# Windowed attention with a linear bias, then a gated layer, on one core: keys in blocks of 32 and four heads to a tile of scores

## The chip, the cores and the metric

The kernel runs on 1 core of one Trainium2 chip. The metric is the device time of the whole program in microseconds (us); lower is better. The engines are TensorE (PE in the profile; PEld is its weight loads), VectorE (DVE), ScalarE (ACT), GpSimd (POOL) and SyncE (SP, which here issues most of the DMAs).

## What is computed

Inputs are q, k and v of shape 4 x 8 x 768 x 64 (batch, heads, sequence, head width), two matrices `moe_w_in` (512 x 1024) and `moe_w_out` (1024 x 512) and a gain `moe_g_ln` of 1024. With `n_global` = 8 and `n_local` = 96:

```
scores = q k^T / 8 - slope(head) * distance        # slope(h) = 2^-(h+1)
keep   = (key < 8) or (0 <= query - key < 96)      # everything else is masked
a      = softmax(scores);   x = a v                # per head, then x as 3072 tokens x 512
h      = x @ w_in;          solu = h * softmax(h)
y      = layernorm(solu) * g_ln;   out = y @ w_out # 3072 x 512, float32
```

A query thus sees at most 96 neighbours and 8 global keys, so that only a band of the 768 x 768 scores has to be computed.

## The kernel before

The program is written out engine by engine. Every piece of work is a *step* (`step(...)`, with its engine, dependencies and buffers); tables of numbers (`ORDER`, `SLOTS`, `ENGS`, `WARM`) give the order in which the steps are issued, the buffer that each takes, the engine where there is a choice, and some matmuls on a constant tile that only keep PE busy at the start. Within one engine, and in SP's queue of DMAs, everything runs in that order.

For each of the 4 batches:

- **Loads.** k and q of a pair of heads come in on SP (`load_heads`, or `load_rows` in runs of 256 bytes), are cast to 16 bits on POOL, DVE or ACT, turned on PE (`turn_k`, `turn_q`, L785: 6 matmuls against the identity) and evacuated on DVE or ACT into `kT`, `qT`. The pairs in `DMAT` (all four of batch 3) are turned by a DMA instead (L829). v comes in on SP (`load_v`) and is cast.
- **Scores.** Keys are cut into blocks of `BLK` = 64. A block's keys are met by `WIN` = 160 queries (64 + 96). A step `scores` takes one pair of heads and 6 blocks: 64 keys of one head on PSUM partitions 0 to 63 and of the other head on 64 to 127, even blocks in one bank, odd blocks in the next (`par`). TensorE is split into four tiles of 64 x 64 (L941). A batch has 8 such steps, 960 columns each for blocks 0 to 5 and 896 for blocks 6 to 11. In batch 0 the bias is added by matmuls with `identb` and `bw` (L927); in batches 1 to 3 (`FACT`) it is multiplied in afterwards by a table `fb` (L959, DVE or POOL). `exp` (L949, ACT) reads both banks at once and writes `eb`.
- **Units.** The 768 queries are cut into two units of 384. For each: scores of the global keys (`gscores`, `gexp` into `eg`), sums over the keys (`sums`, L1027 and L1037: 128 x 32 tiles, one band of 32 partitions for each pair), their logarithm (`ln`, ACT, 384 columns), a split into a high and a low part (`l16`, DVE, L1051), spread over the partitions (`spread`, L1073) and `rexp` (L1085, ACT), which gives the reciprocal.
- **Products with v.** For each duo of pairs (4 heads), `av1` and `av2` (L1121, 64 x 64 tiles) go into one `big` (two PSUM banks). In `av1` two of the tiles take the even blocks and two the odd ones, in `av2` the other way round; a small DVE copy, `tick` (L1129), stands between them. Then `xT` (L1141, DVE) multiplies by the reciprocal into `xT`.
- **The layer.** For each tile of 128 tokens (24 of them): `gemm1` (L1174, 8 matmuls of 512 columns), `ef` (L1180, ACT), `u` (L1183, DVE), squares (L1190 or L1194), a turn of `uu` either on PE (`turn_u`, L1209, evacuated by DVE or ACT) or, for the tiles in `TURNED`, by a DMA (L1199), then `gemm2` (L1266), a scaling (L1276 or L1279) and the store.

PSUM has 8 banks: `acc` is cut into 4 `big` of two banks, which are also used singly as `one`.

Of the kernel before, what the change touches and what calls it, by code (L numbers as in the profile page):

```python
# [18 lines left out]
P = 128  # L19
BLK = 64  # L20
WIN = 160
# [5 lines left out]
TURNED = set(range(5, 22))  # L27
HALVED = {23}
WORDS = {}
DMAT = {(3, p, n) for p in range(4) for n in "kq"}  # L30
# [32 lines left out]
"""  # L63
SLOTS = """
# [10 lines left out]
"""  # L75
ENGS = """
# [5 lines left out]
"""  # L82
WARM = """
20:2:13 32:2:5 45:2:2 54:2:1 82:0:3 100:0:1 110:6:1 139:5:1 171:4:2
# [58 lines left out]
def kernel(  # L143
# [25 lines left out]
    UW = 384  # L169
    RUN = S // P  # L170
    MG = NG + NL
    assert S == 768 and BLK + NL <= WIN and D == 64 and H * NG == 64
# [22 lines left out]
    bw = sb.tile([P, NPR, 3, WIN], FP16, name="bw")  # L195
# [5 lines left out]
    onesg = sb.tile([P, 2, NPR, 32], FP16, name="onesg")  # L201
# [12 lines left out]
    vgz = sb.tile([P, B, H, D], FP16, name="vgz")  # L214
    vt32 = sb.tile([P, B * NPR, D], FP32, name="vt32")
# [12 lines left out]
    v32 = many(3, [P, NBK, D], FP32, "v32_")  # L228
    v16 = many(2, [P, NBK, NPR, D], FP16, "v16_")
# [3 lines left out]
    eg = many(2, [P, UW // 2], FP16, "eg")  # L233
# [27 lines left out]
    def band(p):  # L261

        j = 2 * (p % 2) + p // 2
        return slice(32 * j, 32 * j + 32)

    HW = UW // 2

    def gband(r, p):

        o = 64 * r + 32 * (p // 2)  # L270
        return slice(o, o + 32)
# [13 lines left out]
    sl = sb.tile([P, NPR], FP32, name="sl")  # L285
    sf = sb.tile([P, NPR, 2], FP32, name="sf")
    dm = sb.tile([P, WIN], FP32, name="dm")
    fb = sb.tile([P, NPR, 2, GC], FP16, name="fb")
# [11 lines left out]
    def constants_iota():  # L300
        for hf in HALVES:
            nc.gpsimd.iota(ti[hf], pattern=[[1, WIN]], base=0,
                           channel_multiplier=-1)
            nc.gpsimd.iota(ri[hf, 0:1], pattern=[[0, 1]], base=0, channel_multiplier=1)
        nc.gpsimd.iota(tgm, pattern=[[1, MG]], base=0, channel_multiplier=0)
        nc.gpsimd.iota(ri[:, 1 : 1 + H], pattern=[[NG, H]], base=0, channel_multiplier=0)

    def constants_slopes():
        for p in range(NPR):
            for h, hf in enumerate(HALVES):  # L310
                nc.vector.memset(sl[hf, p : p + 1], -slopes[2 * p + h] / inv_sqrt_d / BSC)

    def constants_factor_slopes():
        for h, hf in enumerate(HALVES):
            for par in range(2):
                for p in range(NPR):
                    nc.gpsimd.memset(sf[hf, p, par : par + 1], -slopes[2 * p + (h ^ par)])

    def constants_factor():
        for p in range(NPR):  # L320
# [37 lines left out]
    def constants_rows():  # L358
        nc.vector.tensor_tensor(out=pick, in0=pick8[:, 0:H], in1=pick8[:, H : 2 * H], op=ALU.add)
        nc.vector.tensor_reduce(out=par4, in_=pick8.rearrange("r (x q l) -> r q x l", q=4, l=2),  # L360
                                axis=AX.XY, op=ALU.add)
        nc.vector.tensor_reduce(out=mlo, in_=pick8.rearrange("r (b l) -> r l b", l=2)[:, 1:2],
                                axis=AX.X, op=ALU.add)
        nc.vector.tensor_scalar(out=sgn, in0=mlo, scalar1=0.25, scalar2=-0.125,
                                op0=ALU.mult, op1=ALU.add)
# [14 lines left out]
    def constants_slr():  # L380
        for h in range(H):
            nc.gpsimd.memset(slr[:, h : h + 1], -slopes[h] * NL)
# [948 lines left out]
```

## Time and profile before

| | |
|---|---|
| time, median of 3 runs | 158.34 us (156.9 to 160.86) |
| the profiled execution | 158.12 us |
| its span, from first to last instruction | 156.5 us |
| busy PE / DVE / ACT / POOL | 144.1 / 119.9 / 123.8 / 51.9 us |
| matmuls | 1974 |
| granted TensorE clock | 1.0 throughout |

Busy time is the share in which at least one instruction of the engine is under way. Matmuls are pipelined and overlap, so a busy PE isn't a PE at its peak. In rows of groups, `x` is the count, then come the busy time in us and the mean duration of one in ns. The chain is the work that ended last, followed back step by step. The span is 1.62 us shorter than the time of the same execution.

### The profile page before, as it was taken

To read this page: it belongs to the slowest core of one execution; us is meant where nothing else is said; L and a number is where in the kernel's file an instruction comes from. 1 tells how busy PE (TensorE), PEld (TensorE's weight loads), DVE (VectorE), ACT (ScalarE), POOL (GpSimd) and SP (SyncE) were. 2 spreads that over 40 slices of the span, in tenths; PEclk is the share of its full clock that TensorE was granted. 3 is DMA by queue.
4 is the path that set the end of the run, shared out by engine and by line. 5 is a ranking of instruction groups with operands and counts; after the bars stand their busy time and mean duration, and the time that the engine had idled before them with its cause. 6 is when DMAs were issued, how large, how long until landed. Compare 5 with 4: busy or idle time off the path is not lost.

```text
span 156.5 us, 4929 instructions
## 1 busy us (share of the span) xinstructions
PE 144.1 (92%) x1974; PEld 76.3 (49%) x1974; DVE 119.9 (77%) x249; ACT 123.8 (79%) x214; POOL 51.9 (33%) x120
## 2 busy tenths in 40 slices
PE   6998986997898999999998999999989799999991
PEld 2455553456454546556544456454444454445460
DVE  6966553799879998889999997499777462788840
ACT  3389986999996999758996998989999546589712
POOL 7705714189438521734960000448301000000000
PEclk9999999999999999999999999999999999999999
DMA  4997899999969999999999899999999983054684
GB/s 157 335 351 178 288 311 397 366 272 329 266 161 264 213 202 294 204 275 201 219 239 176 182 237 216 164 263 135 215 225 290 211 316 133 4 113 89 188 315 168
DMA packets 74317, 35.83 MB, mean 229 GB/s; under 512 B 63344, under 2 KB 69816, under 8 KB 74296
## 3 DMA queue, kind: packets, MB, share of 16 engines
q1 hardware_dynamic: 73576, 34.36, 92.8%
q10 hardware_dynamic: 720, 1.18, 2.0%
q8 instruction: 15, 0.25, 0.6%
q14 instruction: 6, 0.05, 0.1%
HBM read 23.15 MB, written 6.29 MB: 188 GB/s over the span
## 4 chain that ended last, share of the span: by engine, by line
PE 34%; DMA 21%; DVE 16%; SPq 13%; ACT 7%; issue 4%; POOL 3%; DVEq 0%; ACTq 0%; POOLq 0%
PE acc L1266 11%; PE acc L1174 10%; SPq L537 5%; DVE uu L1183 5%; DMA x<-in_k_dram 4%; DVE eb L959 4%; DMA x<-in_q_dram 4%; DMA kT<-x 4%; DMA vgn<-vgn 4%; PE acc L1121 4%; DMA out_dram<-w_out 3%; DVE sqv L1194 3%; SPq L523 3%; SPq L1199 3%; PE acc L785 2%
## 5 line engine op out<-in xcount | busy, mean ns | idle before, releaser
L1174 PE MATMUL acc<-w_in_sb,xT 128*128 128x512 f16 x192 | 44.0, 380 | 1.3 <-POOL w_in_sb L279 1.3
L1266 PE MATMUL acc<-gw_out_sb,late 128*128 128x512 f16 (+1 forms) x200 | 44.7, 371 | 0.0
L1183 DVE SCALAR_TENSOR_TENSOR uu<-ef,acc 128x1024 f16<-128x1024 f16 x24 | 29.1, 1216 | 6.3 <-ACT ef L1180 4.5
L949 ACT ACTIVATE eb<-acc 128x960 f16<-128x960 f32 (+1 forms) x32 | 29.3, 944 | 1.3 <-PE acc L941 1.1
L1180 ACT ACTIVATE ef<-acc 128x1024 f16<-128x1024 f32 x24 | 24.6, 1025 | 6.9 <-PE acc L1174 6.1
L1174 PEld LDWEIGHTS <-xT 128*128 128x128 f16 x192 | 17.8, 98 | 21.5 <-DVE g L625 1.2
L1266 PEld LDWEIGHTS <-late 128*128 128x128 f16 x200 | 18.4, 98 | 20.1 <-issue 0.6
L279 POOL CAST x<-x 128x768 f16<-128x768 f32 x19 | 17.0, 898 | 30.0 <-DMA qT<-x 17.0
L1141 DVE TENSOR_TENSOR xT<-acc,rr 128x768 f16<-128x768 f32 x16 | 15.1, 954 | 5.9 <-ACT rr L1085 4.5
L1276 ACT ACTIVATE w_out<-acc,rstd 128x512 f32<-128x512 f32 (+1 forms) x19 | 12.7, 678 | 7.5 <-PE acc L1266 4.3
L1190 ACT ACTIVATE sqa<-uu 128x1024 f16<-128x1024 f16 x14 | 14.8, 1058 | 1.8 <-DVE uu L1183 1.7
L959 DVE TENSOR_TENSOR eb<-eb,fb 128x960 f16<-128x960 f16 (+1 forms) x21 | 14.8, 735 | 0.0
L1085 ACT ACTIVATE rr<-acc 128x768 f32<-128x768 f32 x16 | 12.2, 805 | 2.9 <-PE acc L1073 2.8
L785 PE MATMUL acc<-ident,x 128*128 128x128 f16 x144 | 11.3, 220 | 2.1 <-POOL x L279 1.1
L1194 DVE SCALAR_TENSOR_TENSOR sqv<-uu 128x1024 f16<-128x1024 f16 x10 | 12.6, 1265 | 0.1
L1121 PE MATMUL acc<-eb,v 64*64 64x160 f16 (+2 forms) x448 | 12.5, 217 | 0.0
L1292 PE MATMUL acc<-busy 128*128 128x512 f16 x29 | 10.3, 485 | 1.5 <-DVE busy L598 1.5
L785 PEld LDWEIGHTS <-x 128*128 128x128 f16 x144 | 8.6, 98 | 5.6 <-POOL x L279 1.5
L1121 PEld LDWEIGHTS <-v 64*64 64x64 f16 x448 | 10.2, 107 | 2.2 <-issue 1.7
L941 PE MATMUL acc<-qT,kT 64*64 64x160 f16 (+2 forms) x384 | 10.8, 227 | 0.3 <-ACT qT L275 0.3
L279 POOL CAST v<-v 128x704 f16<-128x704 f32 (+3 forms) x13 | 6.9, 555 | 11.9 <-DMA v<-in_v_dram 11.9
L1121 PE MATMUL acc<-eg,vgz 64*64 64x192 f16 x128 | 9.2, 257 | 0.0
(113 smaller groups left out, 189.1 us busy)
## 6 DMA issues: line engine op xcount, KB each, us to landing
x<-in_k_dram SPq DMA_DIRECT2D x16, 384.0 KB, 5.8
x<-in_q_dram SPq DMA_DIRECT2D x16, 384.0 KB, 4.8
out_dram<-w_out SPq DMA_DIRECT2D x19, 256.0 KB, 2.9
v<-in_v_dram SPq DMA_DIRECT2D x12, 192.0 KB, 5.3
late<-in_moe_w_in_dram SPq DMA_DIRECT2D x4, 512.0 KB, 4.5
w_out<-in_moe_w_out_dram SPq DMA_DIRECT2D x4, 512.0 KB
v<-in_v_dram SPq DMA_DIRECT2D x12, 160.0 KB, 3.4
v<-in_v_dram SPq DMA_DIRECT2D x12, 96.0 KB, 6.9
```

The lines of the kernel that those rows point to most:

```text
L279: nc.gpsimd.tensor_copy(out=out, in_=in_)
L785: nc.tensor.transpose(out=pt[:, ts(j, P)], in_=a[:, j], identity=ident)
L949: ex["fn"] = (lambda ex=ex, qk=qk, gw=gw: nc.scalar.activation(out=eb[at(qk, "eb")][:, :, 0:gw], in_=big(qk)[:, :, 0:gw], func=AF.Exp, sca ...
L959: eng.tensor_tensor(out=e, in0=e, in1=fb[:, p, :, 0:gw], op=ALU.mult)
L1121: nc.tensor.matmul(out=o_[:, gl : gl + m], lhsT=lhsT, rhs=rhs, start=(ph == 0 and (d, h) not in done), stop=(ph == 1 and last[d, h] == n), ...
L1141: nc.vector.tensor_tensor(out=xT[at(xt_own[b], "xT")][:, p : p + 2, q0:q1], in0=big(av)[:, :, 0:w], in1=rr[at(re, "rr")][:, :, 0:w], op=AL ...
L1174: nc.tensor.matmul(out=ph()[:, ts(fh, 512)], lhsT=xT[at(xt_own[b], "xT")][:, j, ts(t % NA, P)], rhs=w_in_sb[:, j, ts(fh, 512)], start=(j = ...
L1180: ex["fn"] = lambda g1=g1, t=t, ph=ph: nc.scalar.activation(out=ef[at(g1, "ef")], in_=ph(), func=AF.Exp, accum_out=s0[:, t : t + 1])
L1183: u["fn"] = lambda u=u, g1=g1, t=t, ph=ph: nc.vector.scalar_tensor_tensor(out=uu[at(u, "uu")], in0=ef[at(g1, "ef")], scalar=USC, in1=ph(), ...
L1190: nc.scalar.activation(out=sqs_["ACT"], in_=uu[at(u, "uu")], func=AF.Square, accum_out=s2[:, t : t + 1])
L1194: nc.vector.scalar_tensor_tensor(out=sqs_["DVE"], in0=uu[at(u, "uu")], scalar=1.0, in1=uu[at(u, "uu")], op0=ALU.mult, op1=ALU.mult, accum_ ...
L1266: nc.tensor.matmul(out=one(g2)[:, 0:wd], lhsT=uT[at(el_o, "uT")][:, c, :], rhs=gw_out_sb[:, c, sl_], start=(c == 0), stop=(c == NFC - 1))
```

## The change

Keys are cut into blocks of 32, each met by 128 queries (32 + 96). A tile of scores holds four heads, those of pairs dd and dd + 2: 4 x 32 keys on the partitions, even and odd blocks in two banks as before. TensorE is split into eight tiles of 64 x 32 for scores and eight of 32 x 64 for the products with v. A batch still has 8 `scores` steps (4 groups of 6 blocks, 2 tiles each), now 768 columns, and 640 in the last group. The products of all 8 heads of a unit are made together, in two `big`, with one `tick`. The sums of a unit's two halves of 192 queries lie side by side on the partitions, so that `ln` and `l16` have 192 columns. v is loaded in blocks of 64 tokens onto 64 partitions, the one head of a pair shifted by 32 tokens.

With it go new tables of order, buffers and engines; tiles 5 to 7 of the layer are turned on PE instead of by DMA (`TURNED`), and in batch 3 only pairs 1 and 3 are turned by DMA (`DMAT`). Matmuls by form, from the two programs: scores 384 to 816, with `identb` 64 to 64, products with v 576 to 992, sums 224 to 296, spread 32 to 64, turns of q and k 144 to 168, turns of `uu` 56 to 80, on the constant tile 29 to 36. The changes of TensorE's tile form in the order of matmuls are 101 before and 86 now. Exps stay 32.

```diff
-BLK = 64
-WIN = 160
+BLK = 32
+WIN = 128
...
-TURNED = set(range(5, 22))
+TURNED = set(range(8, 22))
...
-DMAT = {(3, p, n) for p in range(4) for n in "kq"}
+DMAT = {(3, p, n) for p in (1, 3) for n in "kq"}
...
-    v32 = many(3, [P, NBK, D], FP32, "v32_")
-    v16 = many(2, [P, NBK, NPR, D], FP16, "v16_")
+    v32 = many(4, [P, NVC + 1, D], FP32, "v32_")
+    v16 = many(2, [P, ND, 2 * NVC + 1, D], FP16, "v16_")
...
-    eb = many(12, [P, 2, GC], FP16, "eb")
-    lns = many(2, [P, UW], FP32, "lns")
-    l16 = many(2, [P, UW], FP16, "l16")
+    eb = many(14, [P, 2, GC], FP16, "eb")
+    lns = many(2, [P, HW], FP32, "lns")
+    l16 = many(2, [P, HW], FP16, "l16")
...
+    def head(duo, d, h):
+
+        return 2 * (duo + 2 * d) + h
...
-    GROUPS_B = [[full(c) for c in range(0, 6)], [full(c) for c in range(6, NBK)]]
-    UNITS_B = [(0, 384, 1), (384, 768, 2)]
+    GROUPS = [[full(c) for c in range(c0, c0 + 6)] for c0 in range(0, NBK, 6)]
+    UNITS_B = [(0, 384, 2), (384, 768, 4)]
...
+    ZONES = [(dd, d, h) for dd in range(ND) for d in range(2) for h in range(2)]
+
+    def av_par(dd, ph):
+
+        return dd ^ ph
...
+                    tiles = [(par, d, h) for par in range(2) for d in range(2) for h in range(2)]
+
+                    def place(par, d, h):
+                        o = 64 * d + 32 * (h ^ par)
+                        return slice(o, o + 32), slice(64 * h, 64 * h + 64)
...
-                            o, r = 64 * (h ^ par), slice(64 * h, 64 * h + 64)
-                            nc.tensor.matmul(
-                                out=sc[o : o + 64, par, col : col + n],
-                                lhsT=kk[r, BLK * c : BLK * c + BLK], rhs=qq[r, g0 : g0 + n],
...
+                            for k_, (c0, q_, m_) in enumerate(todo):
+                                product(t_, kk[d][r, BLK * c : BLK * c + BLK], qq[d][r, q_ : q_ + m_],
+                                        c0, m_, n == len(by[par]) - 1 and k_ == len(todo) - 1)
...
+            moves = [[], []]
+            for gi, c, par, col, n, lo, gl, m in todo:
+                for z in range(2):
+                    a, e = max(gl, HW * z), min(gl + m, HW * z + HW)
+                    if a < e:
+                        moves[z].append((gi, par, col + lo + a - gl, a - HW * z, e - a))
...
-            for duo in [(p, p + 1) for p in range(0, NPR, 2)]:
-                ta = tS + 4500 + 900 * duo[0]
...
+            av = step("PE", av_ns[0], ta, need + [ge, vg_st[b]] + v_need, None,
+                      take=("big", "big"), mode="v", name="av1", lat=330, ni=len(turns[0]))
+            tk = step("DVE", 115, ta + 300, [av], None, lat=95, name="tick")
+            aw = step("PE", av_ns[1], ta + 400, [tk], None, mode="v", name="av2", lat=310,
+                      ni=len(turns[1]))
...
+                    r = BANDS[2 * d + x]
+                    o_ = big(av, dd)[64 * h : 64 * h + 64, d]
```

On DVE, at the products of batch 1 (`tick` is the copy between the two halves of a product, `l` the split logarithm, `xT` the product with the reciprocal). Before:

```order
L1129 COPY tick<-acc 128x1 x2
L1051 SCALAR_TENSOR_TENSOR l_145<-lns_142,mlo 128x384
L1141 TENSOR_TENSOR xT_99<-acc,rr_146 128x2x384
L1141 TENSOR_TENSOR xT_99<-acc,rr_147 128x2x384
L277 CAST x_3_110<-x_4_105 128x768
L1129 COPY tick<-acc 128x1
L277 COPY kT_119<-acc 128x768
L1141 TENSOR_TENSOR xT_99<-acc,rr_146 128x2x384
L277 CAST x_3_110<-x_2_103 128x768
L1129 COPY tick<-acc 128x1
L1141 TENSOR_TENSOR xT_99<-acc,rr_147 128x2x384
```

and now:

```order
L1091 COPY tick<-acc 128x1
L1018 SCALAR_TENSOR_TENSOR l_147<-lns_145,mlo 128x192
L1108 TENSOR_TENSOR xT_99<-acc,rr_150 128x2x384
L1108 TENSOR_TENSOR xT_99<-acc,rr_149 128x2x384
L273 COPY qT_125<-acc 128x768
L1091 COPY tick<-acc 128x1
L1152 SCALAR_TENSOR_TENSOR uu_154,s_93<-ef_152,acc 128x1024
L273 CAST x_2_109<-x_4_105 128x768
L1108 TENSOR_TENSOR xT_99<-acc,rr_150 128x2x384
L1108 TENSOR_TENSOR xT_99<-acc,rr_149 128x2x384
```

There is one `tick` to a unit where there were two, and both products `xT` of a unit follow it.

In SP's queue, where the weights of the first matrix (`late`, four pieces from `in_moe_w_in_dram`) stand among the loads of v for batch 0. Before:

```order
L537 DMA v_0_111<-in_v_dram 128x3x64
L537 DMA v_2_113<-in_v_dram 128x3x64
L552 DMA vgn<-in_v_dram 64x1x64
L658 DMA late<-in_moe_w_in_dram 128x1024 x4
L668 DMA w_out_71<-in_moe_w_out_dram 128x2x512 x4
L537 DMA v_1_112<-in_v_dram 128x3x64
L537 DMA v_1_112<-in_v_dram 128x2x64
```

and now:

```order
L658 DMA late<-in_moe_w_in_dram 128x1024
L534 DMA v_2_113<-in_v_dram 64x6x64
L658 DMA late<-in_moe_w_in_dram 128x1024
L534 DMA v_2_113<-in_v_dram 64x6x64
L534 DMA v_0_111<-in_v_dram 64x6x64
L534 DMA v_1_112<-in_v_dram 64x6x64
L534 DMA v_3_114<-in_v_dram 64x6x64
L534 DMA v_1_112<-in_v_dram 64x6x64
L534 DMA v_3_114<-in_v_dram 64x6x64
L658 DMA late<-in_moe_w_in_dram 128x1024
L668 DMA w_out_71<-in_moe_w_out_dram 128x2x512 x4
```

All of batch 0's v now stands ahead of the last piece of the weights; before, half of it stood behind them.

On ACT, from the logarithms of batch 0 to the first `ef` of the layer. Before:

```order
L1044 ACTIVATE lns_143<-acc 128x384
L1044 ACTIVATE lns_142<-acc 128x384
L275 CAST w_in_sb<-late 128x512
L1085 ACTIVATE rr_146<-acc 128x768
L1085 ACTIVATE rr_147<-acc 128x768
L275 CAST w_in_sb<-late 128x512 x2
L681 ACTIVATE gw_out_sb<-w_out_71,g_73 128x512 x2
L1085 ACTIVATE rr_147<-acc 128x768
L1180 ACTIVATE ef_148,s_92<-acc 128x1024
```

and now:

```order
L1011 ACTIVATE lns_146<-acc 128x192
L1011 ACTIVATE lns_145<-acc 128x192
L271 CAST w_in_sb<-late 128x512
L1097 ACTIVATE rr_149<-acc 128x768
L1097 ACTIVATE rr_150<-acc 128x768
L271 CAST w_in_sb<-late 128x512
L271 CAST v_0_115<-v_3_114 128x384
L1097 ACTIVATE rr_150<-acc 128x768
L271 CAST w_in_sb<-late 128x512
L1097 ACTIVATE rr_149<-acc 128x768
L1149 ACTIVATE ef_152,s_92<-acc 128x1024
```

All four reciprocals of batch 0 now come ahead of the layer's first `ef`; on PE, likewise, both units of batch 0 have their products with v before the first `gemm1`, where the second unit's came after 3 tiles of `gemm1`, the first turns of `uu`, the mean of the weights and some turns and scores of batch 1.

More of the change, by code (lines that the diff above doesn't have):

```diff
@@ L436, in pack @@
         w = max(cols)
-        fill = [(par, cols[par], w) for par in range(2) if cols[par] < w]
-        return got, fill, w
-    PACKED = {b: [pack(g) for g in (GROUPS_A if b == 0 and SPLIT else GROUPS_B)] for b in range(B)}
+        fill = [(x, x[4] + x[2], w) for x in got
+                if x[4] + x[2] == cols[x[3]] and cols[x[3]] < w]
+        return [pack(first[0]), pack(cut), (got, fill, w)] + [pack(g) for g in GROUPS[2:]]
+    PACKED = {b: halves() if b == 0 and SPLIT else [pack(g) for g in GROUPS] for b in range(B)}
     UNITS = {b: UNITS_B for b in range(B)}
@@ L521, in load_heads @@
+        for i, t in order:
+            m = HW if i < 0 else by[av_par(t[0], ph)][i][7]
+            now = max(now, free.get(t, 0))
+            free[t] = now + m / 2.4
+            now += 4
+        return max(free.values()) + 10
     def load_heads(eng, src, dst, b, h0, n, lo, run):
@@ L748, in do_heads @@
                     take=("x32_",), name=nm)
-                assert npr == 1 and lo == 0 and run % 2 == 0
-                p = p0
-                word = WORDS.get((b, p, nm))
-                engs, ns, lats = ("POOL", "DVE", "ACT"), (10 + m, 35 + 0.59 * m, 120 + 0.785 * m), (100, 130, 155)
-                if word:
-                    ns, lats = (ns[engs.index(word)],), (lats[engs.index(word)],)
-                    engs = (word,)
-                cs = step(engs, ns, t0 - 1200, [dma], None, lat=lats,
-                          take=("x16_", dn), free=[(iss, "x32_")], name="cast_" + nm)
@@ L759, in cast @@
-                def cast(cs=cs, iss=iss, word=word):
-                    if word:
-                        copy(cs["at"],
-                             x16[at(cs, "x16_")].rearrange("p (h d j) -> p h d j", h=2, j=run),
-                             x32[at(iss, "x32_")].rearrange("p (h j d) -> p h d j", h=2, d=D))
-                        return
+                p, first = p0, lo == 0
+                cs = step(("POOL", "DVE", "ACT"), (10 + m, 35 + 0.59 * m, 120 + 0.785 * m), t0 - 1200,
+                          [dma] + ([] if first else [own[p, nm][0]]), None, lat=(100, 130, 155),
+                          take=("x16_", dn) if first else ("x16_",), free=[(iss, "x32_")],
+                          name="cast_" + nm)
@@ new lines, in place, with product @@
+                    def place(par, d, h):
+                        o = 64 * d + 32 * (h ^ par)
+                        return slice(o, o + 32), slice(64 * h, 64 * h + 64)
+                    began = set()
+                    def product(t_, lhsT, rhs, c0, m, last):
+                        par, d, h = t_
+                        o, r = place(par, d, h)
+                        nc.tensor.matmul(
+                            out=sc[o, par, c0 : c0 + m], lhsT=lhsT, rhs=rhs,
+                            start=t_ not in began, stop=last,
+                            tile_position=(64 * h, o.start), skip_group_check=True)
+                        began.add(t_)
@@ new lines, in pe @@
+                    by = [[x for x in pieces if x[3] == par] for par in range(2)]
+                    full_ = all(x[1] == 0 and x[4] == WIN * n for y in by for n, x in enumerate(y))
+                    if b not in FACT:
+                        for t_ in tiles:
+                            par, d, h = t_
+                            o, r = place(*t_)
+                            runs = [(0, 0, gw)] if full_ else [(x[4], x[1], x[2]) for x in by[par]]
+                            for c0, a, m in runs:
+                                product(t_, identb[r, 64 * h + 32 * d : 64 * h + 32 * d + 32],
+                                        bw[r, dd].rearrange("r m n -> r (m n)")[:, a : a + m], c0, m, False)
@@ new lines, in sums @@
+                for i in range(max(len(m_) for m_ in moves)):
+                    for dd, z in bands:
+                        if i >= len(moves[z]):
+                            continue
+                        gi, par, col, gl, m = moves[z][i]
+                        j = 2 * dd + z
+                        nc.tensor.matmul(
+                            out=sp[BANDS[j], gl : gl + m], lhsT=onesd[:, par, :],
+                            rhs=eb[at(e_own[b, gi, dd], "eb")][:, par, col : col + m],
+                            start=False, stop=(i == len(moves[z]) - 1),
+                            tile_position=(0, 32 * j), skip_group_check=True)
@@ L1041 @@
             sm["fn"] = sums
-            ln = step("ACT", 50 + 0.84 * w, tS + 1000, [sm], None, lat=165, take="lns", free=[(sm, "one")],
+            ln = step("ACT", 50 + 0.84 * HW, tS + 1000, [sm], None, lat=165, take="lns", free=[(sm, "one")],
                       name="ln")
-            ln["fn"] = lambda sm=sm, ln=ln, w=w: nc.scalar.activation(
-                out=lns[at(ln, "lns")][:, 0:w], in_=one(sm)[:, 0:w], func=AF.Ln)
-            lw = step("DVE", 75 + 1.04 * w, tS + 1800, [ln, rows_st], None, lat=140,
+            ln["fn"] = lambda sm=sm, ln=ln: nc.scalar.activation(
+                out=lns[at(ln, "lns")], in_=one(sm)[:, 0:HW], func=AF.Ln)
@@ L1068 @@
             sp_ = step("PE", 15 + 0.43 * w, tS + 4300, [lw, spr_st], None, take=("big", "big"),
-                       mode="r", name="spread", lat=170, ni=4)
-            def spread(sp_=sp_, lw=lw, w=w):
-                for p in range(NPR):
-                    nc.tensor.matmul(
-                        out=big(sp_, p // 2)[:, p % 2, 0:w],
-                        lhsT=onesr[band(p), p // 2].rearrange("r h d -> r (h d)"),
-                        rhs=l16[at(lw, "l16")][band(p), 0:w],
-                        start=True, stop=True, tile_position=(band(p).start, 0),
-                        skip_group_check=True)
+                       mode="r", name="spread", lat=170, ni=8)
@@ new lines, in spread @@
+            def spread(sp_=sp_, lw=lw):
+                for d in range(2):
+                    for dd in range(ND):
+                        for z in range(2):
+                            j = 2 * dd + z
+                            nc.tensor.matmul(
+                                out=big(sp_, dd)[:, z, HW * d : HW * d + HW],
+                                lhsT=onesr[BANDS[j], d].rearrange("r h d -> r (h d)"),
+                                rhs=l16[at(lw, "l16")][BANDS[j]],
+                                start=(d == 0), stop=(d == 1), tile_position=(32 * j, 0),
+                                skip_group_check=True)
@@ new lines @@
+            av["fn"] = lambda pe=pe: pe(0)
+            aw["fn"] = lambda pe=pe: pe(1)
+            tk["fn"] = lambda av=av, mark=mark: nc.vector.tensor_copy(
+                out=tick, in_=big(av, 1)[:, 1, mark : mark + 1])
+            for dd in range(ND):
+                ta = tS + 4500 + 1800 * dd
+                re = step("ACT", 55 + 2 * w * 0.84, ta, [sp_], None, lat=140, take="rr",
+                          free=[(sp_, dd)], name="rexp")
+                re["fn"] = lambda re=re, sp_=sp_, w=w, dd=dd: nc.scalar.activation(
+                    out=rr[at(re, "rr")], in_=big(sp_, dd)[:, :, 0:w], func=AF.Exp, scale=-1.0)
+                new_x = ui == 0 and dd == 0
```

596 lines of the change are left out of this document (251 added, 345 removed), and 87 rows, old and new, of tables (ENGS, ORDER, SLOTS).

## The prediction

> **What bounds the kernel now.** I read the page's busy times and slices first, then a table by stretch, then what PE waits for, then the chain.
>
> ```profile
> PE 144.1 (92%) x1974; PEld 76.3 (49%) x1974; DVE 119.9 (77%) x249; ACT 123.8 (79%) x214; POOL 51.9 (33%) x120
> DMA  4997899999969999999999899999999983054684
> 25.30:56.00 30.70, 28.22 (x342) 15.30 (x341) 26.04 (x42) 28.52 (x53) 16.22 (x25) 1.00 1.02 272
> 75.00:93.00 18.00, 17.41 (x204) 8.15 (x202) 17.86 (x32) 15.68 (x28) 5.76 (x8) 1.00 1.11 211
> 93.00:124.00 31.00, 29.43 (x442) 14.65 (x434) 23.69 (x52) 26.78 (x47) 8.72 (x10) 1.00 1.18 210
> ```
>
> The last three rows are stretches: length, then busy PE, PEld, DVE, ACT, POOL, granted clock, DMA share, GB/s. From 25.3 us on PE is hardly ever free, but DVE is full from 75 to 93 us, and the DMA engines are full nearly to 130 us. What does PE wait for?
>
> ```profile
> PE acc L927 <- DVE uu L1183: 1.8, 3, 0.7
> PE acc L1174 <- POOL w_in_sb L279: 1.3, 1, 1.3
> PE acc L785 <- POOL x L279: 1.1, 2, 0.6
> PE acc L1027 <- ACT w_out L1276: 0.9, 1, 0.9
> PE acc L785 <- DVE x L277: 0.6, 2, 0.4
> PE acc L1209 <- DVE uu L1183: 0.6, 2, 0.4
> ```
>
> The wait of L1174 is the first `gemm1`. The other five rows make 5.0 us of stalls. Nearly everything else on PE after 25.3 us is work. The chain says so of the end:
>
> ```profile
> 133.12 8.74 PE acc L1174 x40
> ...
> 144.47 8.67 PE acc L1266 x48
> 153.17 0.47 ACT w_out L1276
> ```
>
> So **PE's own work, from its first `gemm1` to the end, plus about 5 us of stalls, sets the time**; what comes before the first `gemm1` is set by loads. I sum the change in these three parts. The first row also gives the price of a column: 40 x 512 columns in 8.74 us, 0.427 ns each.
>
> **PE's work after the first `gemm1`.** Batch 1's attention stands in the chain nearly whole (start, us, what):
>
> ```profile
> 57.13 0.50 PE acc L1027 x16
> 57.63 0.17 PE acc L1037 x8
> ...
> 60.06 0.56 PE acc L1027 x24
> 60.62 0.17 PE acc L1037 x8
> 60.79 0.68 PE acc L1121 x30
> 61.47 0.44 PE acc L785 x6
> 61.91 0.68 PE acc L1121 x30
> ...
> 65.57 0.74 PE acc L1121 x38
> ```
>
> Tiles work side by side: 8 matmuls of L1037 have 192 columns each, 1536 in all, which at 0.427 ns would be 0.66 us one after the other; they take 0.17, as four columns of tiles do. So a step costs the columns of its fullest tile, if all eight tiles of the new form run side by side too.
>
> - *Products with v.* A tile's columns in one of the two halves are, for the first unit, at most 640 (three blocks and 192 global), for the second 672: 0.27 and 0.29 us. A batch has 4 of each: 2.24 us. The new halves have at most 896 and 960 columns, 0.38 and 0.41 us, but hold all 8 heads; a batch has 2 of each, 1.58 us. Saved 0.66 us x 3 batches = 2.0 us. Batch 0's second unit (4 x 0.29 = 1.15 us) moves ahead of the first `gemm1`.
> - *Scores.* 480 columns to a tile now (0.205 us), 384 then (0.164 us). For 24 steps in batches 1 to 3, 1.0 us.
> - *Sums.* Two units: 0.67 + 0.73 us in the rows; the second row group has 896 + 384 columns to a band, 0.55 us, the rest being the change of form and short pieces. Then 768 + 192 columns, 0.41 us. Saved 0.14 us x 6 units = 0.8 us.
> - *Changes of form.* 75 after the first `gemm1` before, 69 now, by the programs' order. One costs about 0.1 us: eight `gemm` matmuls are 1.75 us by the price of a column, and 1.83 to 1.89 where another form follows. Saved 0.6 us.
> - *Turns, added.* Three tiles of `uu` and four of k and q that a DMA turned:
>
> ```profile
> 56.19 0.62 PE acc L1209 x8
> 73.53 0.68 PE acc L785 x12
> 143.58 0.89 PE acc L1209 x16
> ```
>
>   8 cost 0.445 us where no change of form follows, 6 cost 0.34: 3 x 0.445 + 4 x 0.34 = 2.7 us more.
>
> Sum: -2.0 - 1.15 - 1.0 - 0.8 - 0.6 + 2.7 = **-2.85 us**.
>
> **The start.** The first `gemm1` needs all of the first matrix:
>
> ```profile
> 15.72 1.86 SPq L658 DMA_DIRECT2D late<-in_moe_w_in_dram  x4
> 24.67 0.62 ACT L275 CAST w_in_sb<-late 128x512 f16<-128x512 f32 x1 [0.73 <-DMA late<-in_moe_w_in_dram]
> 25.36 0.38 PE L1174 MATMUL acc<-w_in_sb,xT 128*128 128x512 f16 x1 [1.26 <-POOL w_in_sb L279]
> 0.00:25.30 25.30, 21.06 (x350) 11.56 (x351) 17.08 (x55) 18.08 (x25) 13.03 (x68) 1.00 0.87 278
> ```
>
> Its last piece lands just before 24.67 us. Ahead of it stood 0.92 MB of v (8 loads of 96 KB, two of 64 KB for the ends); now all 1.64 MB of batch 0 stand there. 0.72 MB at the 278 GB/s of this stretch is 2.6 us. The DMA engines are 87% busy here, so that up to 13% of 15 us, 2 us, may swallow it; on the other hand the added pieces have runs of 256 bytes. Bounds 0.6 and 4; I take **+2.0 us**, nearer to the row's rate than to the idle share, since SP also issues one by one. The rest of the start I leave even: the first scores, and all of PE's queue behind them, wait for four turned tiles instead of two, which costs at most two loads more (0.77 MB, 2.8 us), but batch 0's exps, which end last there, lose 1.3 us of 7.5:
>
> ```profile
> L949 ACT ACTIVATE eb<-acc 128x960 f16<-128x960 f32 x16 | 15.4, 972 | 0.7 <-PE acc L941 0.6
> L949 ACT ACTIVATE eb<-acc 128x896 f16<-128x896 f32 x16 | 14.6, 916 | 0.6 <-PE acc L941 0.5
> L1085 ACT ACTIVATE rr<-acc 128x768 f32<-128x768 f32 x16 | 12.2, 805 | 2.9 <-PE acc L1073 2.8
> L959 DVE TENSOR_TENSOR eb<-eb,fb 128x896 f16<-128x896 f16 x10 | 8.0, 813 | 0.0
> L959 DVE TENSOR_TENSOR eb<-eb,fb 128x960 f16<-128x960 f16 x11 | 7.2, 664 | 0.0
> ```
>
> **The stalls.** An ACT read of 768 columns of two banks takes 805 ns (L1085), 640 about 0.69 us by the slope of these rows: 24 x 0.805 + 8 x 0.69 = 24.8 us of exps, from 30.0. The multiplications on DVE go from 15.2 us to 12 x 0.53 + 5 x 0.58 = 9.3 (scaled by columns), and 8 `tick`, half of the `l16` columns and 2 squares leave it too: DVE loses some 10 us net of the scalings that it gets. On the DMA side 3 of 17 turns of `uu` and 4 of 8 of k and q go. None of this sets the time by itself. It can shorten the stalls, 2.4 us of which are behind DVE's `uu` and 0.9 behind a store's buffer. I take 3.0 of the 5.0 us away: **-3.0 us**; bounds 0 and -5, and a new wait (below) the other way. Where a stall goes, PE's next piece is a `gemm` whose operands were ready, so nothing else is late there.
>
> **Sum.** 156.5 - 2.85 + 2.0 - 3.0 = 152.65 us of span; with the 1.62 us around it **154.3 us**, against 158.12 of this execution and 158.34 median: 2.5% faster. Under 2% this kernel can't be told from no change.
>
> **The rivals.**
>
> *The start costs its full price and the stalls stay.* 2.6 us at the start, 2.85 off the work, no stall gone: 158.12 + 2.6 - 2.85 = **157.9 us**. For it: full DMA queues to 130 us, and the new order packs the same stores and loads. Against it: a later `gemm1` lets the loads of batch 1 catch up. Chance 0.18.
>
> *All eight banks.* Spread and products of a unit now hold two `big` each, all of PSUM, until the `rexp` and `xT` of the unit are through: 2 x 0.805 (L1085) and two L1141. If PE runs dry for 0.5 us at each of 6 units, 3 us come back: **157.3 us**. Against it: `gemm2` needs one bank only, and `rexp` frees the spread's banks first. Chance 0.15.
>
> *Matmuls have a price of their own.* There are 248 products and 204 scores to a batch after batch 0, 1356 in all. By columns they take 3 x (1.58 + 8 x 0.164) = 8.7 us. If eight tiles can't be fed at 6.4 ns a matmul and it takes 12, they take 16.3 us: +7.6, **161.9 us**, slower; at 9 ns 12.2 us, which eats the gain. From about 10 ns on it decides. What the trace has of short matmuls:
>
> ```profile
> 59.99 0.62 PE L1027 MATMUL acc<-eb,onesd 128*32 128x384 f16 x24
> 60.46 0.34 PE L1037 MATMUL acc<-eg,onesg 128*32 128x192 f16 x8
> ```
>
> 24 matmuls start within 0.47 us; 8 of them have 384 columns on four tiles, 0.33 us; the other 16, of 32 to 96 columns, had 0.14 us, 9 ns each, on four tiles. That is an upper bound for the price with four tiles; with eight it isn't shown. Chance 0.10. The Trainium skill, "TensorE: Matmul & The Clock Gate", section "Wait — 56ns, not 53.3ns?", says that start-to-start never drops below about 25 ns however short a matmul is; by that the 1356 would be an estimated 33.9 us and the kernel some 25 us slower. The 9 ns above speak against it across tiles, so I give it no more than a part of that 0.10.
>
> *More than forecast.* The w_in delay hides in the idle share (0.6) and all stalls go: 158.12 - 2.85 + 0.6 - 5.0 = **150.9 us**. Chance 0.12.
>
> **How the numbers follow.** Forecast 0.45, more than forecast 0.12: faster by over 2% 0.57. Start and banks, within 2%: 0.33. Price of a matmul, slower: 0.10. The range goes from the fast case, 151, to 159, above the two cases of no change and short of the slow one; some 0.1 is left above it and under 0.1 below.
>
> **What would show it.** Products of a unit with v (`av1` or `av2`) in about 0.4 us for 56 or 68 matmuls, and scores at 24 to 0.17 us, would carry the first part; 9 ns or more a matmul would fell it. The first `gemm1` between 26 and 28 us, waiting for `w_in_sb`, carries the start; at 25 I was wrong on the DMA queue. In the table of waits, PE should wait less behind `uu`; a wait of L1174 or of spread behind `xT` or `rr` means banks. DVE near 110 us busy and ACT near 118 carry the sizes. The forecast falls if PE's busy share drops while no engine takes its place, that is, if the new order waits in places that the old one doesn't show.

## The result: slower, and the profile after

The changed kernel takes 172.47 us (median of 4 runs, 170.59 to 175.46) against 157.62 for the kernel before in the same series: a ratio of **1.092, 95% interval 1.077 to 1.107**. The profiled execution took 172.87 us, its span is 171.0, 14.5 more than before. The forecast of 154.3 was wrong, and so was its range. Executions of one kernel differ by several us, and the profiles below of the runs with fewer instructions only, with warming matmuls, of the second order and of merged scores alone are of the longer of their executions, so only differences of several us are read from them.

From the page of the changed kernel: busy time of TensorE, its granted clock and the DMA share in 40 slices of 4.28 us, and the queue that brings instructions.

```profile
PE 149.1 (87%) x2989; PEld 82.6 (48%) x2989; DVE 113.5 (66%) x231; ACT 118.5 (69%) x211; POOL 58.4 (34%) x134
PEclk9999995555999999999999999999999999999999
DMA  4998599999992995899998999999899951179544
q8 instruction: 23, 0.38, 1.1%
```

PE is busy 5 us longer but for a smaller share: it waits more. The clock, 1.0 throughout before, is at half for four slices. The table by stretch (length, busy PE, PEld, DVE, ACT, POOL, clock, DMA share, GB/s) puts that into the start, the waits of PE name what it waited for, and the chain shows it in order of time:

```profile
0.00:25.30 25.30, 18.05 (x430) 9.90 (x434) 9.64 (x37) 14.75 (x23) 15.50 (x79) 1.00 0.81 218
25.30:42.70 17.40, 10.76 (x295) 6.03 (x280) 6.57 (x13) 5.55 (x10) 5.44 (x9) 0.51 1.02 298
```

```profile
PE acc L1003 <- issue: 5.6, 2, 5.4
PE acc L879 <- issue: 2.4, 1, 2.4
...
PE acc L1083 <- issue: 1.4, 3, 0.8
PE acc L879 <- DVE uu L1152: 1.4, 2, 1.1
PE acc L965 <- DVE w_out L1247: 1.0, 1, 1.0
...
PE acc L1234 <- ACT rr L1097: 0.5, 1, 0.5
```

```profile
26.52 5.38 issue
31.90 0.29 PE acc L1003 x5
...
36.93 0.78 issue
37.71 0.52 PE acc L1083 x12
38.46 1.04 PE acc L1083 x44
39.50 3.35 PE acc L1143 x8
```

("issue" is time in which an engine waits for nothing that the profile shows.) The first `gemm1` (L1143) begins at 39.5 us, 25.4 before. Three waits for "issue", 8.6 us, stand ahead of it, all inside a step: in scores (L879), sums (L1003) and products (L1083), between two matmuls with no semaphore between them. The table of before has no wait of PE for "issue".

The first `gemm1` is not quite the same point in both kernels (before, the second unit's products came behind it). The **fifth** nearly is: it begins at 58.8 us, at 48.3 before, with the same work done but for two steps of batch 1's scores (0.29 us each), which the changed kernel makes later. So 10.5 us are lost up to there, and 4.0 from there to the end (112.2 against 108.2). In two runs below whose start is the same, the first `gemm1` came at 36.0 and 37.1 us and the fifth at 55.7 and 56.6: the loss up to the fifth is 7.5 to 10.5 us.

### The profile page after: what moved, and what is told of

The parts are those of the page before. It is cut to its first block, busy times and chain, and to the rows that moved or that the text cites. A ratio compares the mean times of both kernels' runs of the same rounds, so it can differ in the third digit from the quotient of the medians.

```text
span 171.0 us, 6933 instructions
## 1 busy us (share of the span) xinstructions
PE 149.1 (87%) x2989; PEld 82.6 (48%) x2989; DVE 113.5 (66%) x231; ACT 118.5 (69%) x211; POOL 58.4 (34%) x134
## 4 chain that ended last, share of the span: by engine, by line
PE 49%; DMA 13%; ACT 10%; issue 9%; DVE 8%; SPq 8%; POOL 0%; DVEq 0%; ACTq 0%
PE acc L1234 18%; PE acc L1143 16%; PE acc L1083 7%; DMA out_dram<-w_out 4%; SPq L534 4%; DMA x<-in_k_dram 3%; DVE uu L1152 3%; DMA late<-uu 3%; DVE eb L923 3%; PE acc L768 2%; DMA late<-in_moe_w_in_dram 2%; ACT sqa L1159 2%; PE acc L879 2%; PE acc L1003 2%; ACT kT L271 2%
## 5 line engine op out<-in xcount | busy, mean ns | idle before, releaser
L1143 PE MATMUL acc<-w_in_sb,xT 128*128 128x512 f16 x192 | 45.8, 389 | 0.0
L1234 PE MATMUL acc<-gw_out_sb,late 128*128 128x512 f16 (+1 forms) x200 | 44.8, 371 | 0.5 <-ACT rr L1097 0.5
L1234 PEld LDWEIGHTS <-late 128*128 128x128 f16 x200 | 18.4, 98 | 20.1 <-issue 1.1
L1143 PEld LDWEIGHTS <-xT 128*128 128x128 f16 x192 | 17.9, 100 | 20.6 <-issue 2.3
L913 ACT ACTIVATE eb<-acc 128x768 f16<-128x768 f32 (+1 forms) x32 | 24.0, 789 | 3.0 <-PE acc L879 2.9
L1159 ACT ACTIVATE sqa<-uu 128x1024 f16<-128x1024 f16 x16 | 17.0, 1061 | 2.7 <-DVE uu L1152 2.6
L275 POOL CAST v<-v 128x768 f16<-128x768 f32 (+3 forms) x15 | 11.1, 750 | 18.6 <-DMA v<-in_v_dram 18.4
L879 PE MATMUL acc<-qT,kT 64*32 64x128 f16 (+3 forms) x816 | 11.2, 214 | 4.2 <-issue 2.4
L1083 PE MATMUL acc<-eb,v 32*64 32x128 f16 (+3 forms) x864 | 12.3, 228 | 1.7 <-issue 1.4
L1260 PE MATMUL acc<-busy 128*128 128x512 f16 x36 | 11.6, 456 | 1.5 <-DVE busy L600 1.5
L1083 PEld LDWEIGHTS <-v 32*64 32x64 f16 x864 | 10.7, 113 | 4.1 <-issue 3.9
L879 PEld LDWEIGHTS <-kT 64*32 64x32 f16 x816 | 8.5, 91 | 8.5 <-issue 6.2
L1018 DVE SCALAR_TENSOR_TENSOR l<-lns,mlo 128x192 f16<-128x192 f32 x8 | 3.3, 418 | 13.7 <-ACT lns L1011 13.7
L923 POOL TENSOR_TENSOR eb<-eb,fb 128x768 f16<-128x768 f16 (+1 forms) x7 | 11.2, 1608 | 3.1 <-ACT eb L913 3.1
L1244 ACT ACTIVATE w_out<-acc,rstd 128x512 f32<-128x512 f32 (+1 forms) x13 | 8.4, 654 | 5.5 <-PE acc L1234 4.3
```

What stands on the lines that cost most here:

```text
L275: nc.gpsimd.tensor_copy(out=out, in_=in_)
L879: nc.tensor.matmul(out=sc[o, par, c0 : c0 + m], lhsT=lhsT, rhs=rhs, start=t_ not in began, stop=last, tile_position=(64 * h, o.start), ski ...
L913: ex["fn"] = (lambda ex=ex, qk=qk, gw=gw: nc.scalar.activation(out=eb[at(qk, "eb")][:, :, 0:gw], in_=big(qk)[:, :, 0:gw], func=AF.Exp, sca ...
L923: eng.tensor_tensor(out=e, in0=e, in1=fb[:, dd, :, 0:gw], op=ALU.mult)
L1083: nc.tensor.matmul(out=o_[:, gl : gl + m], lhsT=lhsT, rhs=rhs, start=(ph == 0 and t not in done), stop=(ph == 1 and last[t] == n), tile_po ...
L1143: nc.tensor.matmul(out=ph()[:, ts(fh, 512)], lhsT=xT[at(xt_own[b], "xT")][:, j, ts(t % NA, P)], rhs=w_in_sb[:, j, ts(fh, 512)], start=(j = ...
```

## The experiments

**Theory A: instructions.** PE's program comes in packets of 16,384 bytes through the DMA engines, which are full in the start. The change raised PE's instructions from 3949 to 5979 (15 and 23 such packets), and attention uses them up quickly. **Theory B: data.** v, global values and `w_in` come later in the new order of loads. **Theory D: a matmul has a price of its own.** The packets in the trace against PE's standstills:

```
             PE stands (us)    packet (us)      restart behind packet's end
changed      21.64 - 24.06     21.60 - 22.64    1.42
             26.52 - 31.90     29.03 - 30.43    1.47
             36.93 - 37.71     35.45 - 36.41    1.30
```

Between the first and the second restart PE makes exactly 256 instructions, and a packet holds 256 of 64 bytes. By the count, a packet is asked for when the 256 ahead of the last ones are used up: from that point to its start it took 5.0, 3.6 and 4.0 us between 24 and 42 us (mean DMA share 1.02), up to 3.0 us from there to 130 us (1.09), and 0.6 to 1.2 us for the next four (0.62 behind 130 us). So a full DMA share goes with longer waits, but does not set their length alone. Then 0.9 to 1.8 us for the packet itself and 1.3 to 1.5 until PE goes on. The Trainium skill, "Runtime: NRT & Kernel Launch", section "Instruction fetch mechanics", describes the same blocks of 256 instructions and calls their cost mostly hidden; the size agrees, the rest doesn't hold here: 5.38 us for one.

**More instructions in the kernel before.** Each matmul of scores and products of batch 0 in three pieces:

```diff
+    k_ = 3 if b == 0 else 1
...
-        out=sc[o : o + 64, par, col : col + n],
...
+    for y in range(k_):
+        y0, y1 = n * y // k_, n * (y + 1) // k_
...
+            out=sc[o : o + 64, par, col + y0 : col + y1],
...
```

> The kernel before, but in batch 0 each matmul of scores and of products with v is cut into three of a third of the columns: 480 more matmuls and weight loads, the same columns, data, loads and waits. PE has 4909 instructions instead of 3949. Theory A (supply of instructions): waits for 'issue' of 3 to 8 us appear on PE in the start, each ending 1 to 2 us after the end of a packet of the instruction queue; the first gemm1 at 31 us or later instead of 25.4; span 163 us or more. Theory B (data late): the loads are those of before, so only the price of the matmuls themselves comes in, at most 10 ns each where the columns don't cover it: first gemm1 at 28.5 us at most, span 161 us at most.

Measured 176.97 us (before 159.03; ratio 1.116, 1.087 to 1.144), first `gemm1` at 37.0 us. PE's waits in the first 38 us, and two places of the chain:

```profile
PE acc L1127 <- issue: 6.2, 2, 4.0
PE acc L927 <- issue: 2.7, 1, 2.7
```

```profile
25.58 2.20 issue
27.78 0.52 PE acc L1127 x32
...
30.01 3.96 issue
33.97 0.42 PE acc L1127 x6
```

The packets ended at 26.31 and 32.57 us; PE went on 1.47 and 1.40 us later. With the loads of before and no new form of tile, instructions alone move the first `gemm1` by 11.6 us; the 480 matmuls themselves can be 4.1 of these (at 8.6 ns each, below). Its fifth `gemm1` begins at 68.7 us, and from there it takes 107.6 us, as before (108.2). Theory A holds.

**Fewer instructions, less data, both.** Three runs leave out one or the other in the changed kernel:

```diff
+    if b == 0 and n < max(len(y) for y in by) - 1:
+        continue                        # two of three key products
...
+    if b == 0:                          # products: global keys and the joint only
+        turns = [[x for x in turns[0][:-2] if x[0] < 0] + turns[0][-2:], ...]
```

> The changed kernel, but batch 0 leaves out 336 of its matmuls: of the three key products of each tile of scores only the last is made (the bias stays), and of the products with v only those of the global keys and the four at the joint of the two halves. All loads, casts, exps and waits stay. PE has 5307 instructions instead of 5979. Theory A (PE runs out of instructions in the start, because they come in pieces of 16 KB, 256 instructions, behind full DMA engines): the waits for 'issue' before the first gemm1 fall from 7.8 us to under 2, the granted clock stays at 1.0, the first gemm1 comes at 29 us or earlier instead of 39.5, the span is 161 us or less. Theory B (data of the start come late: the order of loads on SP and the full DMA engines hold scores, global values or w_in): only the work that is left out is saved, 336 matmuls at 11 ns, 3.7 us; the first gemm1 not before 35 us, the span 167 us or more.

```diff
-    take=() if first else ("v32_",), name="v")
+    take=() if first else ("v32_",), name="skip" if b == 0 and i == 1 else "v")
```

> The changed kernel without the eight loads of the second halves of v in batch 0 and their casts; batch 0's products take blocks of the first halves in their place, so that all matmuls stay. SP has the last piece of w_in some 6 us earlier. If the data of the start alone set the first gemm1 (theory B), it comes at 28 us or earlier instead of 36 to 39.5. If the supply of instructions alone does (theory A), it stays at 32 us or later, with waits for 'issue' of 4 us or more in sum ahead of it, each ending 1.3 to 1.9 us after the end of a packet of the instruction queue.

> Both: batch 0 without 336 of its matmuls (as in the run with fewer matmuls at the start) and without the second halves of v. With the fewer matmuls alone the first gemm1 came at 32.4 us, behind the cast of v and the last piece of w_in, and no wait for 'issue' stood ahead of it. If supply and data together are the whole delay of the start, the first gemm1 comes at 28 us or earlier now, with under 1 us of waits for 'issue' ahead of it. If it stays above 30, something third holds the start (banks, exps, or the chain of sums, logarithm and spread).

```
                          first gemm1   fifth gemm1   time, median (us)
kernel before                25.4          48.3         157.6
changed                      39.5          58.8         172.5
less data only               38.6          57.7         175.1
fewer instructions only      32.4          53.1         171.5
both                         28.1          48.8         165.4
```

With less data alone the waits for "issue" stay (7.4 us) and the first `gemm1` hardly moves. With fewer instructions none is left in the table of waits ahead of it, but it comes at 32.4 us, between my two bounds: PE now waits for data, and SP's queue says why.

```profile
PE acc L1088 <- ACT v L271: 3.0, 1, 3.0
PE acc L1088 <- POOL vgz L563: 2.4, 1, 2.4
```

```profile
20.50 0.60 SPq L658 DMA_DIRECT2D late<-in_moe_w_in_dram  x1
21.15 6.21 SPq L534 DMA_DIRECT2D v<-in_v_dram  x6
27.41 0.61 SPq L658 DMA_DIRECT2D late<-in_moe_w_in_dram  x1
```

(Start, length, what.) Six loads of v take SP 6.2 us to issue (four of about 0.6, then 1.2 and 2.3), and the last piece of `w_in` stands behind them; before, all four pieces were issued between 15.7 and 17.6 us. So **A and B lie side by side, and the later one shows**: B holds the first `gemm1` to 32.4 us, A to 36 to 39.5. Without both it is 28.1, and the fifth comes at 48.8, near that of before; of the gain, the 336 matmuls left out are some 2.9 us by themselves (at 8.6 ns).

**The clock.** In that last run it still fell to half from 25.3 to 32.2 us, with waits of PE of only 0.4 to 0.8 us. Eight matmuls on the constant tile into these:

```diff
-80:3:2 130:5:3
+80:3:2 106:6:4 107:2:2 118:4:2 130:5:3
```

> The run with fewer matmuls in batch 0 and fewer loads of v (first gemm1 at 28.1 us, clock at half from 25.3 to 32.9 us, eight matmuls of the first gemm1 in 3.39 us), with eight more matmuls on the constant tile where PE waits between 20 and 25 us. If the clock falls because PE waits there, it stays at 1.0 now: eight matmuls of gemm1 take 1.73 us, and the span is 3 to 5 us shorter, 159 to 161 us. If the waits of PE are not what lowers it, clock and span stay as they were (164.1), or 1 us longer.

The clock lines of the two runs' pages, without the warming matmuls and then with them:

```profile
PEclk9999995599999999959999999999999999999999
```

```profile
PEclk9999999999999999879999999978999999999999
```

The start is at full clock, eight matmuls of the first `gemm1` take 1.74 us instead of 3.39, the fifth `gemm1` comes at 47.7: here the half clock is a follow-up of PE's waits. The span did not fall by the 3 to 5 us expected (165.4 us, 162.7 in the other execution, against 164.1 and 163.0 without these matmuls): 1.1 us were gained up to the fifth `gemm1` and lost behind it, where PE waited 5.7 us for "issue" in `gemm2`. The Trainium skill, "TensorE: Matmul & The Clock Gate", section "Part 1: The HAM clock gate (the "warmup" mystery)", ties the clock to how busy PE was lately; these two runs agree.

**Does the DMA load delay the packets?** First, all loads behind `w_in` held back:

```diff
+    if s["i"] == 145:                   # first load of w_out
+        nc.vector.memset(w_out32[:, 0, 0:1], 0.0)   # and three more pieces
```

> The changed kernel, with four one-column memsets on DVE into the w_out tile, in DVE's order behind the first unit's product with the reciprocal: SP can issue the w_out loads, and all loads behind them, only then, so that the DMA engines empty after the last piece of w_in. PE's instructions, and all loads that the first gemm1 needs, stay as they are. Theory A: the packet of instructions that PE waits for at 26 us comes 2 to 4 us earlier, the wait for 'issue' in the sums falls from 5.4 us to under 3, and the first gemm1 comes at 36.5 us or earlier; batch 1 may start later. Theory B (data of the start late) and a price of the matmuls: the first gemm1 stays at 39 us within 1, since nothing ahead of it moved.

The first `gemm1` came at 36.0 us with a wait of 2.9, as expected, 173.89 us in all. But it came at 36.0 and 37.1 us too in the next two runs, whose start is untouched (waits of 2.0 and 3.6 in the sums): the wait changes that much by itself, and this run tells nothing. The next two do: 456 more matmuls of half the columns, in batch 2 and in batch 3.

```diff
+    k_ = 2 if b == 2 else 1             # pieces of a matmul; the other run: b == 3
```

> The changed kernel, but in batch 2 each matmul of scores (key products) and of products with v is cut into two of half the columns: 456 more matmuls and weight loads, the same columns. PE has 6891 instructions instead of 5979. Theory A (supply): batch 2 takes 3.6 pieces of 16 KB more, and PE waits for 'issue' 4 us or more in sum between 85 and 125 us where it waited 1.5; span 5 to 10 us longer than the changed kernel. Theory D (each matmul has a price of its own of 8 to 9 ns, whatever its columns): 48 scores take 0.75 to 0.85 us for 96 instead of 0.38, 3.9 us more in all, without waits for 'issue'. If columns alone cost: no change of PE's work in a step.

> The changed kernel with scores and products of batch 3, not batch 2, cut into two of half the columns: again 456 more matmuls, the same columns, but most of them where the DMA engines are half idle (after 130 us). If a packet of instructions is late because it stands behind other transfers, the waits for 'issue' are shorter here than the 11 us that the same cut cost in batch 2: 2 to 6 us, and the span grows by 6 to 9 us over the changed kernel's. If the time of the packet itself or PE's own queue sets it, whatever else the DMA engines do, it is again 10 us or more, and the span grows by 12.

185.07 and 179.05 us. PE's waits in batch 2 (84 to 133 us) of the one, and from 112 us on of the other:

```profile
PE acc L879 <- issue: 5.0, 3, 3.0
PE acc L1089 <- issue: 5.0, 3, 3.5
```

```profile
PE acc L1089 <- issue: 1.9, 2, 1.4
PE acc L1006 <- issue: 1.3, 1, 1.3
PE acc L879 <- issue: 0.7, 1, 0.7
```

Ten microseconds against four for the same instructions (the times grew by 12.6 and 6.6 us; of the four, 1.4 stand ahead of 130 us): packets are later where the DMA engines are full (share 1.03 from 84 to 133 us of the one, 0.45 behind 130 us of the other). They also give the price of a matmul. Scores of the changed kernel, and then of the split one, as they stand in the two timelines (the next instruction starts at 56.39 and at 89.02 us):

```profile
55.85 0.60 PE L879 MATMUL acc<-qT,kT 64*32 64x128 f16 x48
```

```profile
88.07 1.02 PE L879 MATMUL acc<-qT,kT 64*32 64x64 f16 x96
```

48 in 0.54 us, 96 of half the columns in 0.95: 0.416 us before rounding for 48 more, **8.6 ns each**, though the columns are the same. The kernel before had for the same two steps (next instruction at 77.06 us)

```profile
76.54 0.59 PE L941 MATMUL acc<-qT,kT 64*64 64x160 f16 x24
```

0.52 us: no gain. Theory D holds, at 8 to 9 ns.

**Can the order be mended?** `w_in` ahead of the second halves of v, the second unit's products behind two `gemm1`; in the third run the bias by two full matmuls:

```diff
+    move([138, 126, 130], 134)          # next two runs: behind 30
+    move([188, 241, 242, 243, 254, 251], 714)
```

> The changed kernel, the whole computation, with two places moved back to where the kernel before had them: SP issues the four pieces of w_in together, ahead of the second halves of v, and PE makes the products with v of batch 0's second unit behind the first two gemm1 (the second of these in another pair of banks). PE's instructions are the same in number. The data part of the delay should go: w_in is cast by 28 us, and the first gemm1 comes 3 to 6 us earlier than in the changed kernel with the same waits for 'issue' in the sums, at 30 to 34 us, and span 2 to 5 us below the changed kernel's. If supply alone set the start, the first gemm1 comes at most 2 us earlier.

With this edit the small loads of global values stood behind `w_in` too, and the products waited 4.6 us for `vgz`. First `gemm1` 36.9, 176.24 us.

> The reordered kernel with its slip mended: w_in's pieces together behind the four small loads of global values of v (which the first products wait for), not ahead of them. Whole computation, the same number of instructions on PE as in the changed kernel. In the run before it, the global values were late (a wait of 4.6 us of the first products). Data and supply together: that wait goes, w_in is cast by 28 us, waits for 'issue' of 3 to 8 us stay ahead of the first gemm1, which comes at 30 to 34 us; span 166 to 170 us.

> The same, and batch 0's bias is added by two matmuls over the whole array to a step of scores (with a permuted identity) instead of eight on tiles: 48 matmuls and as many weight loads fewer ahead of the first gemm1, for 1.3 us more of columns in a stretch where PE waits anyway. Whole computation. If the supply of instructions holds the rest of the start, the waits for 'issue' ahead of the first gemm1 shrink by 1.5 us or more against the run without this edit, and it comes that much earlier, at 28 to 32 us. If not, it comes no earlier, or 0.5 to 1.3 us later for the columns.

First `gemm1` at 34.6 and 33.2 us, waits for "issue" ahead of it 5.8 and 4.3 us, 1.5 us apart as expected for 96 instructions fewer; but waits differ by that much between equal starts, so this is not shown. But 176.03 (173.71 to 178.34) and 178.73 us in all: the fifth `gemm1` is at 59.5 and 58.6, where it was. The unit's work that was moved back has to be made there anyway, with its own waits. The spans that I expected were wrong; neither version beats the kernel before.

**The rest.** All three key products of a tile as one matmul of the same columns, first alone, then on top of the run with warming matmuls:

```diff
-    product(t_, kk[d][r, BLK * c : BLK * c + BLK], qq[d][r, q_ : q_ + m_], ...)   # three
+    product(t_, kk[d][r, BLK * c : BLK * c + BLK], qq[d][r, q_ : q_ + gw], 0, gw, True)
```

> The changed kernel, but in all four batches the three key products of each tile of scores are made as one matmul over all columns of the tile, with one block of keys: the same columns, 560 matmuls and weight loads fewer (PE 4859 instructions instead of 5979), everything else as it was. Theory A (supply of instructions): less than 4 us of waits for 'issue' ahead of the first gemm1 instead of 8.6, which comes at 36 us or earlier, under 1.5 us of such waits behind it, and the span is 5 to 10 us below 171, 161 to 166. Price of a matmul alone (8 ns for one of 128 columns, of which 6.8 are its columns): 560 matmuls give at most 1.5 us. Columns alone: no change.

> The run with extra matmuls on the constant tile (batch 0 with fewer products, without the second halves of v), with the scores of all batches made as one matmul to a tile: PE 4459 instructions. There the fifth gemm1 came at 47.7 us (48.3 in the kernel before), but waits for 'issue' of 7.7 us stood behind it, in gemm2 and turns. If supply is what keeps the rest of this kernel from being shorter than the kernel before, those waits fall under 1.5 us and the stretch from the fifth gemm1 to the end goes from 117.7 us to 109 or less (108.2 before); the span to 157 or less. If something else sets the rest (DMA transfers, DVE, the added turns), it stays above 113.

The first gained what was expected in the start (waits for "issue" of 2.4 us ahead of the first `gemm1`, which came at 33.0 us; the fifth at 52.6) and kept next to none of it: 6.1 us of such waits stood behind it, where I expected under 1.5, and it took 171.74 us. The second took 163.1 us, 1.031 of before (1.020 to 1.042), its fifth `gemm1` at 46.9, the rest 114.4 us, not 109. PE's time from the fifth `gemm1` to the end, summed from start to start by kind of work (gaps over 0.1 us apart; the row of `gemm2` holds the 3.1 to 3.3 us behind the last matmul; the row of scores is 19 steps before and 21 in the others):

```
us                       before   changed   merged   merged, start mended
products with v             9.0       8.4      8.5       8.3
scores                      5.4       6.1      4.9       5.0
sums, spread, gscores       7.3       7.0      7.2       6.8
turns of k, q and uu        4.9       8.3      8.2       8.1
gemm1                      35.4      35.5     35.5      37.7
gemm2 and the end          43.2      42.5     44.1      42.3
gaps                        3.1       4.5      9.2       6.3
together                  108.2     112.2    117.5     114.4
```

So the supply of instructions isn't all of the rest. The **added turns cost 3.4 us** (by this count; no run takes them out), attention as a whole saves 0.3 with two more steps of scores in it, `gemm2` saves 0.45 and the end 0.25, gaps add 1.4. A step of scores takes 0.28 us before and 0.29 now. In the last run one wait for "issue" is left, 3.8 of the 6.3 us of gaps, and it is the supply again (of the 7.7 us that I counted as such in the run with warming matmuls alone, 2.0 were a wait behind DVE, and are still there):

```profile
64.77 0.27 PE acc L1041 x6
65.04 3.82 issue
68.86 0.34 PE acc L1041 x2
```

Its packet came at 65.71 to 67.22 us, 4.6 us after its turn, with 1520 instructions fewer in the program; 2.3 us of `gemm1` go with it, at half clock. Why such waits move from run to run, and grow in the rest when the start gets shorter, stays open; what the DMA queues hold when a packet is asked for may set it, but no run here shows that.

## Why the prediction was wrong, point by point

- **Where the miss lies.** The span missed by 18.3 us. Up to the fifth `gemm1` the forecast comes to +0.85 (2.0, less 1.15 for the products that move ahead of the layer), and 10.5 came; from there on it comes to -4.7, and +4.0 came. The start is the larger part, the other terms nearly half.
- **The start, +2.0 us, is the step that failed first**: +14.1 at the first `gemm1`, +10.5 at the fifth, where both kernels have done nearly the same work. I priced the added v by its bytes, and called the rest of the start even. The bytes were not the price; the place of the last piece of `w_in` in SP's queue was: it was issued at 28.65 us, at 17.2 before, behind six loads of v that took 5.5 us to issue. That is some 7 us (25.4 to 32.4 us in the run with fewer instructions). I had read the order of SP's queue and not added up the time of its issues. And I never asked where PE's instructions come from: 2030 more of them were written in front of me, with 15 packets of a queue "instruction" on the page. No rival had that, so the range missed as well.
- **The stalls, -3.0 us, didn't go.** PE waits less behind `uu` (1.4 from 2.4 us), but 1.0 still behind a store's buffer, and 1.2 us of waits for "issue" stand behind the fifth `gemm1`, where there were none. Gaps from there on went from 3.1 to 4.5 us: 4.4 us off, the largest miss outside the start.
- **PE's work, -2.85 us, failed in size.** The halves of products take 0.48 and 0.57 us from first to last, not 0.38 and 0.41; in batches 1 to 3 that saves 0.6 us, not 2.0. Sums and spread save 0.3, not 0.8. Scores cost the same per step (0.29 against 0.28 us) instead of 1.0 us less in all. Products and scores are the rival "matmuls have a price of their own", which I held at 0.10 and which came true at 8.6 ns, where I had said that 9 eats the gain: by its own sum 1356 of them are 11.7 us for 8.7 of columns, and these two terms came out 2.5 us above the forecast. `gemm2` took 0.45 us less, where I had 0.6 for changes of form; that these are its cause is not shown. The turns cost 3.4 where I had 2.7.
- The 25 ns from start to start of the Trainium skill, "TensorE: Matmul & The Clock Gate", section "Wait — 56ns, not 53.3ns?", would have cost an estimated 25 us more; with eight tiles the runs show 8.6 ns. The trace's 9 ns for four tiles was the better witness.
- **All eight banks**: no wait of L1143 behind `xT` or `rr` is among PE's waits, but `gemm2` (L1234) waits once behind `rr`, 0.5 us, which may be a bank that the spread held. It is a sixth of the 3 us that this rival had.
- **Sizes elsewhere**: ACT 118.5 us busy (118 forecast), DVE 113.5 (110). These were right, and set nothing.
- The sentence that fell due was the last one: PE's busy share dropped (92 to 87%) and no engine took its place.

## What to carry to other kernels

Count a program's instructions on each engine, not only its columns: two for each matmul, 256 to a packet, and in the start of the changed kernel a packet took 6 to 8 us to be of use (3.6 to 5.0 of waiting, 1.0 to 1.4 of transfer, 1.3 to 1.5 to restart). Work that uses up 256 instructions in less (128 small matmuls: 1.1 us at 8.6 ns) should stand between long matmuls or be cut into fewer and longer ones, most of all where loads fill the queues; the runs with merged scores show it for the start only, and no run here made the whole kernel faster than before. And add up a queue of DMA issues in order, with its stops (six loads of v: 5.5 and 6.2 us), up to the transfer that the critical step waits for.

## What the runs showed that was not expected

- A wait named "issue" inside a step, with no semaphore, ended 1.3 to 1.5 us after the end of an instruction packet in all three cases of the changed kernel's start and in those of the kernel before with split matmuls.
- Issuing six loads of v on SP took 5.53 us in the changed kernel and 6.21 in the run with fewer instructions: most took 0.6 us each, but one took 2.15 in the first, and two 1.2 and 2.3 in the second.
- The clock fell to half even without a long wait (four of 0.4 to 0.8 us within 5 us), and 8 more matmuls on a constant tile kept it up, in one execution each.
